# One output DMA per result tile, with a re-ordered first stage, in a fused attention and hard-swish MLP kernel

## Chip, cores and metric

The kernel runs on one core of a Trainium2 chip. The metric is device time in microseconds (us). The kernel before was timed three times; the profile is one further execution. A core has five engines, each with a queue of its own that is worked through in order: TensorE (PE, with its weight loads as PEld), VectorE (DVE), ScalarE (ACT), GpSimd (POOL), and SyncE (SP), which here only issues DMA transfers. The transfers are carried out by 16 DMA engines.

## What is computed

Cosine attention over 8 batches of 12 heads (448 positions, 64 channels), and then a two-layer MLP on the 3,584 tokens:

```python
q_n = q / (norm(q, axis=-1) + 1e-6)          # q, k, v: (8, 12, 448, 64) float32
k_n = k / (norm(k, axis=-1) + 1e-6)
attn = softmax(q_n @ k_n.T / tau)
x = (attn @ v) -> (8 * 448, 12 * 64)
h = x @ w_in                                 # (768, 2048)
g = h * clip(h + 3, 0, 6) / 6
out = g @ w_out                              # (2048, 768), out: (3584, 768) float32
```

## The kernel before

The work is cut into 48 **pairs** of heads, six to a batch. For each pair, q and k are loaded (`LQ`, line 174), squared (`SQ`, 203 or 201), summed (`RE`, 215), turned into reciprocal norms on ACT (`NO`, 231 to 234), multiplied (`NM`, 246), and transposed, on PE (`TR`, 291) in the first pairs and by a DMA transpose later (`XD`, 302). PE makes the scores in four groups (`SC`, 394), ACT the exponentials (`EX`, 412), PE the product with v (`VA`, 433), DVE the division (`FI`, 448). The result goes back into channel-major form by PE (`BK`, 466, with a copy `CX`) or by a DMA transpose (`XB`, 480). v is loaded by `LV` (four transfers, 186) and cast by `VC`.

When the six pairs of a batch are in `xT`, the first product of the MLP can run: 16 **units** per batch of six matmuls each (`mm1_unit`, 496), with a Relu on ACT (505) and a product on DVE (511) behind each. The second product is 56 units of 16 matmuls (`mm2_unit`, 532). One such unit makes a tile of 128 tokens by 384 columns. `store` copies it out of PSUM into `o` (543 on ACT, 545 on DVE, in turn; four buffers) and sends it to `out`. The weights come in eight transfers issued by POOL (`W`, 591).

The 128 rows of a tile are not consecutive tokens. Token `7 p + c` of a batch sits at place `p` of chunk `c`, and a tile holds two chunks of 64 tokens, so its rows lie 7 rows apart in `out`, in two groups. For tiles 0 to 2 of a batch the groups are two neighbouring chunks of one batch; tile 3 (odd batches only) takes chunk 6 of two batches. The kernel before sends each group by a DMA of its own:

```python
for e in range(2):
    ...
    eng = nc.scalar if end == 1 and e else nc.sync
    eng.dma_start(out=r[:, cols], in_=o[64 * e : 64 * e + 64, 0:width])
```

The last unit of all is cut into two halves of 192 columns, and one of its four transfers is issued by ACT.

The order of the work is written out by hand. For pairs 0 to 17, `PLAN` is a list of short names (`SQ.1.a.0.4` is a square of item 1 on ACT, `U` one MLP unit, `UA` and `UV` its ACT and DVE halves, `DP.n` a run of n matmuls on zeros that keep PE occupied). Each engine executes its share in the order of this list. `ORDER` says which kind of unit (first or second product) each of the first 36 `U` takes. From pair 18 on (`FIRST`) a loop emits one pair after the other: scores, exponentials, the values of the pair before, `XB`, `XD`, units, loads.

Of the kernel before, what the change touches and what calls it, by code (L numbers as in the profile page):

```python
# [15 lines left out]


FIRST = 18
ORDER = "111111111111111111111111111112212222"

PLAN = [
    "DP.4 LQ.1 DP.2 SQ.1.a.11.3 SQ.1.a.0.4 LQ.0 DP.2 LQ.3 SQ.1.a.4.3 DP.5 LQ.2 SQ.0.a.8.6 SQ.0.p.6.2 DP.4",
    "SQ.1.v.7.4 SQ.0.p.0.6 DP.3 RE.1.1 RE.1.0 RE.0.1 DP.1 NO.0.1 LQ.5 DP.4 RE.0.0 SQ.3.a.0.7 DP.2 NO.0.0 NM.1.v.0",
    "NM.0.p.1 DP.8 NM.1.v.1 SQ.2.a.0.7 RE.3 LQ.4 SQ.5.a.0.7 TR.1.Y DP.11 RE.2 NM.0.p.0 SQ.4.p.0.7 CK.0.v TR.0.Z",
    "NO.1 DP.2 CQ.0.v SC.0.0.0 RE.5 DP.3 DP.2 EX.0.0 SC.0.1.1 EX.0.1 DP.3 SC.0.2.0 LV.0 LQ.8 CK.1.v RE.4 LQ.7",
    "EX.0.2 CQ.1.v VC.0.p NM.2.p LQ.6 DP.6 SC.0.3.1 VA.0.0 NM.3.p LV.1 VC.1.v VA.0.1 SC.1.0.0 EX.0.3 VA.0.2 TR.2.Z",
    "VA.0.3 DP.3 SC.1.1.1 LV.2 NO.2 EX.1.0 FI.0 TR.3.Y SC.1.2.0 LQ.9 EX.1.1 NM.4.p CK.2.v VA.1.0 EX.1.2 CQ.2.v",
    "VA.1.1 VC.2.v SC.1.3.1 CQ.3.v NM.5.p SQ.7.p.0.7 SC.2.0.0 DP.2 EX.1.3 VA.1.2 EX.2.0 SC.2.1.1 EX.2.1 CK.3.v",
    "VA.1.3 SC.2.2.0 TR.4.Y BK.0.Z FI.1 SC.2.3.1 DP.2 EX.2.2 DP.1 EX.2.3 CQ.4.v SQ.6.p.0.7 W CX.0.v SC.3.0.0",
    "EX.3.0 CQ.5.v RE.7 TR.5.Z VC.3.v SC.3.1.1 VA.2.0 W VA.2.1 EX.3.1 VA.2.2 VA.2.3 RE.6 CK.4.v SQ.9.a.0.7",  # L30
    "SC.3.2.0 EX.3.2 SC.3.3.1 D.10 LQ.10 LQ.11 SC.4.0.0 CK.5.v FI.2 VA.3.0 NO.3 RE.9 SQ.8.p.0.7 NM.7.p EX.3.3",
    "BK.2.Z RE.8 EX.4.0 SC.4.1.1 VA.3.1 EX.4.1 SC.4.2.0 VA.3.2 EX.4.2 BK.1.Y CX.2.v VA.3.3 SC.4.3.1 LV.3 SC.5.0.0",
    "VC.4.v NM.6.p DP.2 EX.4.3 SC.5.1.1 EX.5.0 TR.7.Z CX.1.v TR.6.Y LV.4 EX.5.1 FI.3 SC.5.2.0 VC.7.p VA.4.0 EX.5.2",
    "VC.6.v CK.6.v NO.4 SC.5.3.1 VA.4.1 EX.5.3 VA.4.2 VC.5.p CS.6.v VA.4.3 DP.5 CQ.6.v CQ.7.v SQ.11.p.0.7 OPEN",
    "SQ.10.p.0.7 CS.7.v CK.7.v FI.4 RE.11 SC.6.0 SC.6.1 EX.6.0 EX.6.1 BK.3 SC.6.2 VA.5.0 NM.8.p VA.5.1 EX.6.2",
    "CX.3.v VA.5.2 VA.5.3 FI.5 SC.6.3 SC.7.0 SC.7.1 TR.8 XB.4 EX.6.3 VA.6.0 LQ.13 VA.6.1 EX.7.0 RE.10 NM.9.p",
    "SC.7.2 EX.7.1 CQ.9.v VA.6.2 EX.7.2 BK.5 TR.9 CQ.8.v LQ.14 CX.5.v SC.7.3 VA.6.3 VC.9.p CK.9.v U NO.5 FI.6 U U",
    "UA UA VA.7.0 EX.7.3 VA.7.1 UA CS.9.v UV W CS.8.v CK.8.v SC.8.0 UV UV SC.8.1 NM.10.p VA.7.2 VA.7.3 FI.7 EX.8.0",
    "SC.8.2 LQ.12 VC.8.p W EX.8.1 TR.10 U LV.5 EX.8.2 UA VA.8.0 CQ.11.v SC.8.3 SQ.13.p.0.7 VA.8.1 CQ.10.v UV",
    "SC.9.0 SC.9.1 EX.8.3 NM.11.p EX.9.0 RE.13 VA.8.2 SC.9.2 VA.8.3 FI.8 EX.9.1 SC.9.3 LQ.15 EX.9.2 U UA TR.11",  # L40
    "SQ.12.p.0.7 EX.9.3 RE.12 CS.11.v VA.9.0 VA.9.1 VC.10.p U CK.10.v XB.6 NO.6 NM.12.p VC.11.p SQ.15.p.0.7",
    "CK.11.v SC.10.0 CS.10.v UV VA.9.2 U UA SC.10.1 EX.10.0 UV UA EX.10.1 SC.10.2 VA.9.3 EX.10.2 LV.6 U UV UA",
    "TR.12 LQ.17 LQ.16 CQ.12.v XB.7 SC.10.3 U SQ.14.p.0.7 NM.13.p UV CQ.13.v SC.11.0 UA RE.15 FI.9 EX.10.3 EX.11.0",
    "U U UV UA UA VA.10.0 SC.11.1 EX.11.1 UV SC.11.2 EX.11.2 VA.10.1 UV VA.10.2 TR.13 SC.11.3 LQ.19 U LV.7 CS.12.a",
    "UA VA.10.3 RE.14 NO.7 SQ.17.p.0.7 NM.15.p CS.13.v CK.13.a U U FI.10 EX.11.3 UA VA.11.0 VA.11.1 VA.11.2",
    "NM.14.p SQ.16.a.0.7 UA CK.12.v SC.12.0 RE.17 XB.8 UV W U VA.11.3 VC.12.p U UV UV EX.12.0 FI.11 SC.12.1 UA",
    "XB.9 UV VC.15.p UA UV EX.12.1 LQ.18 SC.12.2 XB.10 VA.12.0 BK.11 SC.12.3 SC.13.0 EX.12.2 CX.11.v VA.12.1 XD.15",
    "U EX.12.3 EX.13.0 SC.13.1 SC.13.2 UA W U EX.13.1 VA.12.2 RE.16 SQ.19.p.0.7 VC.13.a VA.12.3 EX.13.2 UV SC.13.3",
    "UA U XD.14 FI.12 NO.8 UV SQ.18.p.0.7 CK.14.v U U EX.13.3 U VA.13.0 UA UV SC.14.0 UA UA UA EX.14.0 UV CS.14.v",
    "VC.14.a UV UV SC.14.1 EX.14.1 U SC.14.2 UA NM.16.v RE.19 UV EX.14.2 VA.13.1 U UA U W VA.13.2 UA RE.18 UV UV",  # L50
    "CK.15.v U LQ.20 SC.14.3 UA NO.9 XD.16 UV LQ.21 VA.13.3 U FI.13 U U NM.17.p XD.17 XB.13 UA VA.14.0 UV VA.14.1",
    "SC.15.0 UA EX.14.3 XB.12 VA.14.2 LV.8 UV UA UV EX.15.0 VA.14.3 SC.15.1 W EX.15.1 SC.15.2 FI.14 SQ.21.a.0.7",
    "CK.16.v EX.15.2 SC.15.3 SQ.20.a.0.2 U EX.15.3 U VA.15.0 SQ.20.p.2.5 VA.15.1 NM.19.v RE.20 UV SC.16.0 VC.17.v",
    "CS.16.v SC.16.1 UA CK.17.v SC.16.2 XD.19 EX.16.0 VC.16.v VA.15.2 RE.21 LQ.22 VA.15.3 U EX.16.1 EX.16.2",
    "SC.16.3 FI.15 UA NM.18.p U UV U XD.18 EX.16.3 UA NO.10 VA.16.0 VA.16.1 SC.17.0 SQ.22.p.0.7 SC.17.1 LV.9",
    "VC.18.p UV CK.18.v RE.22 EX.17.0 SC.17.2 VA.16.2 NM.20.v LV.11 XB.14 EX.17.1 VA.16.3 U LQ.23 VC.19.a SC.17.3",
    "UA U EX.17.2 FI.16 XB.16 UV CK.19.v LV.10 CS.18.v EX.17.3 VA.17.0 XB.15",
]


# [1 line left out]
def kernel(  # L62
# [10 lines left out]
    nc = tc.nc  # L73
    B, H, S, D = q.shape
    d_model, d_ff = moe_w_in.shape
# [194 lines left out]
    def bank_of(name, reads):  # L270

        bank = {"Y": Y, "Z": Z}[name] if name else next_bank()
        key = id(bank)
        assert not unread.get(key), name
        unread[key] = reads
        return bank, key
# [246 lines left out]
    def mm2_unit(b, t, m, end=None):  # L523
        assert not weights
        g = gT[(b // 2) % 2]
        ps, key = bank_of(None, 1)
        width = MH if end is None else MH // 2
        cols = slice(m * MH + width * (end or 0), m * MH + width * (end or 0) + width)
        for fc in range(FCN):
            c0 = (S + SR) * (b % 2) + 128 * t if t < 3 else SM  # L530
            lhs = g[:, fc, c0 : c0 + 128]
            nc.tensor.matmul(  # L532
                ps[:, 0:width],
                lhs,
                w_out_sb[:, fc, cols],
                start=(fc == 0),
                stop=(fc == FCN - 1),
            )

        def store():  # L540
            o = sb.tile([128, MH], FP32, name="o", tag="o", bufs=4)
            if on_act:
                nc.scalar.copy(out=o[:, 0:width], in_=ps[:, 0:width])  # L543
            else:
                nc.vector.tensor_copy(out=o[:, 0:width], in_=ps[:, 0:width])  # L545
            unread[key] = 0
            for e in range(2):
                if t < 3:
                    r = out[b * S : (b + 1) * S].rearrange("(p c) m -> c p m", c=7)[2 * t + e + b % 2]
                else:  # L550
                    r = out[(b - 1 + e) * S : (b + e) * S].rearrange("(p c) m -> c p m", c=7)[6 * (1 - e)]
                eng = nc.scalar if end == 1 and e else nc.sync
                eng.dma_start(out=r[:, cols], in_=o[64 * e : 64 * e + 64, 0:width])

        evac_n[0] += 1
        on_act = evac_n[0] % 2 == 1
        post["a" if on_act else "v"].append(store)

    def second(b):
# [107 lines left out]
    SC = [psum_s.tile([128, 2, 512], FP32, name=f"SC{n}", tag=f"SC{n}") for n in range(2)]  # L667
# [3 lines left out]
    by_kind = {"1": [u for u in stream if u[0] is mm1_unit], "2": [u for u in stream if u[0] is mm2_unit]}  # L671
    first = [by_kind[x].pop(0) for x in ORDER]
    stream = first + [u for u in stream if u not in first]
# [91 lines left out]
```

## Time and profile before

| | before |
|---|---|
| timed runs | 428.23 us median (426.42, 428.23, 429.01) |
| profiled run | 424.55 us; 422.8 us from the first to the last instruction |
| PE busy | 411.1 us, 97% of the span |
| ACT, DVE, POOL busy | 271.2, 217.7, 181.1 us |
| output transfers | 110 of 96 KB and 4 of 48 KB, 2.2 us to landing |
| read from and written to memory | 47.19 MB and 11.01 MB |

The page lists each engine's busy time, the same in 40 slices of the span, and the chain of work that ended last. A group line reads: source line, engine, operation, output from inputs, count, then busy time and the mean duration in ns. A windows line gives a stretch of time, then for each engine its busy time and the instructions, then the granted TensorE clock, the mean busy share of the 16 DMA engines, and the rate in GB/s at which they moved data.

### The profile page before, as it was taken

To read this page: it belongs to the slowest core of one execution; us is meant where nothing else is said; L and a number is where in the kernel's file an instruction comes from. 1 tells how busy PE (TensorE), PEld (TensorE's weight loads), DVE (VectorE), ACT (ScalarE), POOL (GpSimd) and SP (SyncE) were. 2 spreads that over 40 slices of the span, in tenths; PEclk is the share of its full clock that TensorE was granted. 3 is DMA by queue.
4 is the path that set the end of the run, shared out by engine and by line. 5 is a ranking of instruction groups with operands and counts; after the bars stand their busy time and mean duration, and the time that the engine had idled before them with its cause. 6 is when DMAs were issued, how large, how long until landed. Compare 5 with 4: busy or idle time off the path is not lost.

```text
span 422.8 us, 9251 instructions
## 1 busy us (share of the span) xinstructions
PE 411.1 (97%) x3574; PEld 243.2 (58%) x3575; DVE 217.7 (52%) x419; ACT 271.2 (64%) x593; POOL 181.1 (43%) x184
## 2 busy tenths in 40 slices
PE   6999999999997999999999999999999999999996
PEld 5556655556654555656555555555555555655564
DVE  7689777675443454465455454554554343214410
ACT  6899989977555765866756775676765675105400
POOL 5997787512235456365365464374472200000000
PEclk9999999999999999999999999999999999999999
DMA  8997999996879767676995856668666251330033
GB/s 287 307 244 201 243 194 226 220 194 145 210 170 203 174 175 138 167 194 127 179 193 136 183 156 156 158 154 188 164 160 95 63 75 33 70 75 19 2 75 76
DMA packets 94156, 65.82 MB, mean 156 GB/s; under 512 B 58656, under 2 KB 92576, under 8 KB 94112
## 3 DMA queue, kind: packets, MB, share of 16 engines
q1 hardware_dynamic: 90320, 58.89, 60.4%
q0 software_dynamic: 3712, 6.29, 8.7%
q8 instruction: 28, 0.46, 0.5%
q14 instruction: 16, 0.13, 0.1%
q10 hardware_dynamic: 80, 0.05, 0.0%
HBM read 47.19 MB, written 11.01 MB: 138 GB/s over the span
## 4 chain that ended last, share of the span: by engine, by line
PE 88%; ACT 4%; DMA 4%; SPq 2%; issue 1%; POOL 0%; DVE 0%; ACTq 0%; POOLq 0%
PE M L496 22%; PE M L532 22%; PE PV L433 11%; PE Y L496 6%; PE M L394 6%; PE Z L496 5%; PE Y L532 5%; PE Z L532 5%; ACT at L412 3%; DMA tT<-nrm 2%; PE Z L394 2%; DMA raw<-in_k_dram 1%; PE SC L394 1%; PE Y L394 1%; PE PV L603 1%; DMA vr<-in_v_dram 1%
## 5 line engine op out<-in xcount | busy, mean ns | idle before, releaser
L532 PEld LDWEIGHTS <-gT 128*128 128x128 bf16 x912 | 88.7, 98 | 58.6
L412 ACT ACTIVATE at<-M 128x448 bf16<-128x448 f32 x195 | 94.9, 568 | 30.5 <-PE M L394 25.3
L496 PEld LDWEIGHTS <-w_in_sb 128*128 128x128 bf16 x768 | 74.1, 98 | 67.1 <-issue 3.4
L532 PE MATMUL M<-w_out_sb,gT 128*128 128x384 bf16 (+1 forms) x640 | 106.0, 322 | 0.0
L496 PE MATMUL M<-xT,w_in_sb 128*128 128x448 bf16 x510 | 104.2, 352 | 0.0
L246 POOL TENSOR_TENSOR nrm<-raw,r 128x896 bf16<-128x896 f32 (+1 forms) x45 | 74.2, 1655 | 26.6 <-ACT r L234 22.9
L203 POOL TENSOR_TENSOR sq<-raw 128x896 f32<-128x896 f32 (+3 forms) x42 | 67.8, 1618 | 28.9 <-DMA raw<-in_k_dram 11.6
L511 DVE SCALAR_TENSOR_TENSOR gT<-u,M 128x448 bf16<-128x448 bf16 x85 | 52.5, 621 | 51.0 <-ACT u L505 49.8
L505 ACT ACTIVATE u<-M,half_bias 128x448 bf16<-128x448 f32 x85 | 55.1, 652 | 20.9 <-PE M L496 19.5
L433 PEld LDWEIGHTS <-at 128*128 128x128 bf16 x1344 | 53.3, 98 | 24.9 <-issue 17.7
L433 PE MATMUL PV<-vx,at 128*128 128x65 bf16 (+1 forms) x1344 | 63.9, 198 | 0.0
L215 DVE TENSOR_REDUCE n<-sq 128x14 f32<-128x896 f32 (+1 forms) x50 | 51.9, 1041 | 3.4 <-POOL nrm L246 2.0
L351 POOL COPY km<-tT 64x128 bf16<-64x128 bf16 x34 | 10.6, 312 | 94.1 <-DVE rc L448 33.7
L543 ACT COPY o<-M 128x384 f32<-128x384 f32 (+1 forms) x21 | 9.9, 471 | 40.9 <-PE M L532 40.9
L449 DVE TENSOR_TENSOR on<-PV,rc 128x512 bf16<-128x512 f32 x48 | 33.2, 692 | 3.5 <-DMA xT<-on 1.9
L545 DVE COPY o<-M 128x384 f32<-128x384 f32 (+1 forms) x19 | 10.4, 547 | 47.7 <-PE M L532 47.7
L394 PE MATMUL M<-tT,kz 64*128 64x448 bf16 (+1 forms) x172 | 33.4, 353 | 1.4 <-DMA tT<-nrm 0.5
L412 ACT ACTIVATE at<-Y 128x448 bf16<-128x448 f32 x48 | 27.4, 571 | 10.9 <-PE Z L394 10.9
L412 ACT ACTIVATE at<-Z 128x448 bf16<-128x448 f32 x51 | 29.0, 569 | 3.0 <-PE M L394 2.7
L496 PE MATMUL Y<-xT,w_in_sb 128*128 128x448 bf16 x138 | 29.9, 352 | 0.0
L448 DVE RECIPROCAL rc<-PV 128x8 f32<-128x8 f32 x48 | 9.9, 206 | 38.2 <-PE PV L433 34.9
L496 PE MATMUL Z<-xT,w_in_sb 128*128 128x448 bf16 x120 | 26.1, 352 | 2.0 <-DMA xT<-on 2.0
(78 smaller groups left out, 342.8 us busy)
## 6 DMA issues: line engine op xcount, KB each, us to landing
vr<-in_v_dram SPq DMA_DIRECT2D x96, 128.0 KB, 3.8
raw<-in_k_dram SPq DMA_DIRECT2D x24, 448.0 KB, 4.4
raw<-in_q_dram SPq DMA_DIRECT2D x24, 448.0 KB, 4.3
out_dram<-o SPq DMA_DIRECT2D x110, 96.0 KB, 2.2
w_in_sb<-in_moe_w_in_dram POOLq DMA_DIRECT2D x4, 768.0 KB, 12.1
w_out_sb<-in_moe_w_out_dram POOLq DMA_DIRECT2D x4, 768.0 KB, 11.2
xT<-on SPq DMA_TRANSPOSE x42, 3.8
tT<-nrm SPq DMA_TRANSPOSE x34, 2.9
```

What stands on the lines that cost most here:

```text
L203: engines[e].tensor_tensor(out=o, in0=i, in1=i, op=ALU.mult)
L215: nc.vector.tensor_reduce(out=n2s[d % 2][:, j % 2, c], in_=sq[:, :, :, :].rearrange("p g c d -> p (g c) d")[:, c, :], axis=AX.X, op=ALU.add,)
L246: engines[e].tensor_tensor(out=nrm[:, :, g, :].rearrange("p c g d -> p g c d"), in0=raw_of[j][:, g, :, :], in1=rs[d % 2][3][:, j % 2, :] . ...
L351: nc.gpsimd.tensor_copy(out=km[p, :, p], in_=z[p, 3, :, :])
L394: nc.tensor.matmul(o, ks, qt[rows], start=True, stop=True)
L412: nc.scalar.activation(out=o, in_=x, func=AF.Exp, scale=inv_tau)
L433: nc.tensor.matmul(o, at[:, n, q_cols(i // HP, j)], mv, start=(name == "A0" and j % 2 == 0), stop=last, skip_group_check=True,)
L449: nc.vector.tensor_tensor(out=on[:, :, :, :].rearrange("p (b j) h d -> p b (j h) d", b=2), in0=pv4[:, :, :, 0:D], in1=rc[:, :, :].to_broad ...
L496: nc.tensor.matmul(ps[:, 0:S], w_in_sb[:, cc, fc * 128 : (fc + 1) * 128], x[:, cc, 0:S], start=(cc == 0), stop=(cc == CC - 1),)
L505: nc.scalar.activation(out=u[:, :], in_=ps[:, 0:S], func=AF.Relu, bias=half_bias[:, :], scale=1.0 / 6.0)
L511: nc.vector.scalar_tensor_tensor(out=g[:, fc, c0 : c0 + S], in0=u[:, :], scalar=1.0, in1=ps[:, 0:S], op0=ALU.min, op1=ALU.mult,)
L532: nc.tensor.matmul(ps[:, 0:width], lhs, w_out_sb[:, fc, cols], start=(fc == 0), stop=(fc == FCN - 1),)
```

## The change

The two output transfers of a tile become one, whose destination is written as an access pattern with the two groups as its outermost dimension. `step` is the distance between the groups: one row for two neighbouring chunks, `S - 6` rows for the tile that spans two batches. All of them are issued by SyncE. What it is for: half as many output transfers to issue. The plan for pairs 0 to 17 is also replaced by another order of the same work, found by a search that took several lengths for the transfers.

```diff
-ORDER = "111111111111111111111111111112212222"
+ORDER = "111111111111111111111111111111222222"
 PLAN = [
-    "DP.4 LQ.1 DP.2 SQ.1.a.11.3 SQ.1.a.0.4 LQ.0 DP.2 LQ.3 SQ.1.a.4.3 DP.5 LQ.2 SQ.0.a.8.6 SQ.0.p.6.2 DP.4",
-    "SQ.1.v.7.4 SQ.0.p.0.6 DP.3 RE.1.1 RE.1.0 RE.0.1 DP.1 NO.0.1 LQ.5 DP.4 RE.0.0 SQ.3.a.0.7 DP.2 NO.0.0 NM.1.v.0",
-    "NM.0.p.1 DP.8 NM.1.v.1 SQ.2.a.0.7 RE.3 LQ.4 SQ.5.a.0.7 TR.1.Y DP.11 RE.2 NM.0.p.0 SQ.4.p.0.7 CK.0.v TR.0.Z",
+    "LQ.0 SQ.0.p.0.6 DP.2 DP.4 DP.1 LQ.1 DP.7 DP.2 DP.2 SQ.1.p.7.4 DP.5 SQ.0.v.6.2 DP.2 SQ.0.a.8.6 DP.3 D.10 LQ.2",
+    "DP.3 RE.0.1 SQ.1.a.4.3 RE.0.0 LQ.3 LQ.5 LQ.4 SQ.1.a.0.4 SQ.1.v.11.3 NO.0.0 RE.1.0 SQ.2.p.0.7 RE.1.1 RE.2",
+    "NM.0.p.0 LQ.6 DP.5 NM.0.p.1 LV.0 SQ.3.a.0.7 TR.0.Z NO.0.1 SQ.4.a.0.7 NM.1.p.0 RE.3 NM.1.v.1 DP.4 NO.1 CQ.1.v",
     ...
 ]
 ...
-            for e in range(2):
-                if t < 3:
-                    r = out[b * S : (b + 1) * S].rearrange("(p c) m -> c p m", c=7)[2 * t + e + b % 2]
-                else:
-                    r = out[(b - 1 + e) * S : (b + e) * S].rearrange("(p c) m -> c p m", c=7)[6 * (1 - e)]
-                eng = nc.scalar if end == 1 and e else nc.sync
-                eng.dma_start(out=r[:, cols], in_=o[64 * e : 64 * e + 64, 0:width])
+            c = 2 * t + b % 2 if t < 3 else 6
+            row = b * S + c if t < 3 else (b - 1) * S + c
+            step = 1 if t < 3 else S - 6
+            r = bass.AP(
+                tensor=out.tensor,
+                offset=out.offset + row * d_model + cols.start,
+                ap=[[step * d_model, 2], [7 * d_model, 64], [1, width]],
+            )
+            nc.sync.dma_start(out=r, in_=o[:, 0:width])
```

In the rest of the new plan the `XB` of pairs 1 and 2 stand in place of PE's `BK` of 1 and 2, `BK` of pairs 4 and 8 in place of `XB` of 4 and 8, and the weight transfers `W` come earlier. The number of `U` is 36 in both plans, and the loop from pair 18 on is unchanged.

## The prediction

> **What bounds the kernel now.** I read the page's busy times first, then PE's waits, then the chain in order of time, and last the DMA engines by stage.
>
> PE's waits, from the list of who waited for whom (engine and line, what it waited for, us in total, times, longest):
>
> ```profile
> PE Z L496 <- DMA xT<-on: 2.0, 1, 2.0
> PE M L394 <- DMA tT<-nrm: 0.5, 1, 0.5
> ```
>
> The page has PE busy for 97%, but in the first 41 us many of its matmuls are the zero runs of lines 603 and 598 (77 and 9 of them), which compute nothing. The first unit of the MLP starts at 41 us; until then ACT is busy 23.5 of the 25 us from 15 to 40. From 136 us to the last matmul at 419 us PE streams without a gap: a first-product unit takes 1.14 us, a second-product unit 2.60, again and again in the chain. So PE's own work sets the end, plus what PE loses before 136 us. The two waits above are the whole of the loss after 126 us. Both are for transfers that SyncE issued late. Its timeline (start us, us, line, operation, transfer, count) has no gap from 99 to 127 us:
>
> ```profile
> 119.21 1.17 SPq L553 DMA_DIRECT2D out_dram<-o  x2
> 120.43 2.67 SPq L186 DMA_DIRECT2D vr<-in_v_dram  x4
> 123.15 1.28 SPq L480 DMA_TRANSPOSE xT<-on  x1
> 124.47 0.59 SPq L174 DMA_DIRECT2D raw<-in_k_dram  x1
> 125.17 1.20 SPq L480 DMA_TRANSPOSE xT<-on  x1
> ```
>
> The last line is the transpose that PE waits for until 129.1 us. The 12 output transfers issued between 99.3 and that line held SyncE for 8.6 us (3.67 + 1.17 + 1.19 + 1.42 + 1.17).
>
> The DMA engines by stage (stretch, five engines' busy time, clock, **DMA share**, **GB/s**):
>
> ```profile
> 5.00:10.00 5.00, 4.32 (x42) 3.54 (x40) 4.34 (x8) 4.41 (x13) 2.13 (x4) 1.00 1.03 380
> ```
>
> ```profile
> 100.00:160.00 60.00, 57.38 (x496) 33.76 (x492) 28.79 (x51) 36.45 (x84) 23.43 (x23) 1.00 0.74 179
> 160.00:320.00 160.00, 160.00 (x1388) 94.13 (x1385) 81.07 (x144) 107.07 (x243) 83.47 (x80) 1.00 0.72 163
> 320.00:361.00 41.00, 41.00 (x350) 23.96 (x348) 16.76 (x32) 26.29 (x56) 6.22 (x9) 1.00 0.40 61
> ...
> 400.00:423.00 23.00, 19.04 (x133) 12.35 (x131) 2.03 (x4) 2.23 (x5) 0.00 (x0) 0.97 0.28 70
> ```
>
> The reader should see two prices. From 5 to 10 us only loads run: 380 GB/s over 16 engines busy 1.03 of the time is 380 / 16.5 = 23.1 GB/s for an engine while it is busy. From 400 us on only outputs run: 70 / (16 x 0.28) = 15.6 GB/s. And from 100 to 320 us the engines are already busy for 0.72 to 0.74 of the time with everything spread over all 16.
>
> [...] when loads pile up at 38 to 57 us, a transpose of `xT` issued at 42.77 lands 15.2 us later, against a median of 3.8. [...] Issue time is what merging saves here: the trace has about 0.6 us for each transfer.
>
> **The change part by part.**
>
> *Fewer issues.* 114 output transfers become 57. Ahead of the late transpose six of 12 go, about 4.3 us of SyncE time. It is issued at 120.9 in place of 125.2 and lands at about 124.8, while PE wants it at 127. Both waits go: 2.0 + 0.5, with the gaps around them 2.8 us. Elsewhere SyncE's time is hidden behind PE.
>
> *The merged transfer.* Its destination has dimensions 2 x 64 x 384, its source 128 x 384. [...] each output tile runs on **two DMA engines** in place of 16, the same two each time, 64 rows of 1,536 bytes (98.3 KB) on each. At 23.1 GB/s that takes 98.3 / 23.1 = 4.26 us, at 15.6 GB/s 6.3 us. The trace shows no write at such a width, so these are my two bounds. I take 4.5 us, near the lower, since the 15.6 was measured with 16 engines writing at once and here two do.
>
> *Those two engines from 100 us to 361 us.* 42 of the 56 units of the second product lie there (84 transfers before). Their outputs need 42 x 4.5 = 189 us of each of the two engines. The rest of the traffic still takes its sixteenth. Upper bound from busy shares: 60 x 0.74 + 160 x 0.72 + 41 x 0.40 = 176 us per engine, less the outputs' part before (84 x 98.3 KB = 8.26 MB at 15.6 GB/s over 16 engines = 33 us), is 143 us. Lower bound from bytes at the loads' rate: 10.7 + 26.1 + 2.5 - 8.3 = 31 MB, over 16 engines at 23.1 GB/s, 84 us. I take the middle, 113.5. Sum 302.5 us in a stretch of 261: 41.5 us too much. The four `o` buffers allow four tiles of backlog (18 us), which drain from 361 to 400 us, where only six units store. The other 23.5 us reach PE, in two ways: the copies behind the second product wait for a free `o`, on ACT and DVE in turn, and behind them in those queues stand exponentials and Relus, for which PE waits; and loads and transposes, which need all 16 engines, stand in the rings behind outputs. This is **+23.5 us**.
>
> *The end.* From 398 us the last eight units run at 2.60 us each, faster than two engines take their tiles. Of the 2.2 us to landing now, 98.3 KB at 16 x 15.6 GB/s are 0.4 and latency 1.8. So the first store moves from 402.9 (matmuls done 400.6, copy 0.5, latency 1.8). Seven tiles x 4.5 and two halves x 2.3 make 36.1 us, so the last lands at 439.0, against 421.7 before: **+17 us**. PE is done by then.
>
> *The new order.* The same 36 units and within 1 us the same work on ACT, DVE and PE by its end; weights leave earlier and two of the early transposes move from PE to DMA. On POOL a full square (line 203, 1.68 us) now stands ahead of the first products with the norms, and ACT squares item 4, whose load lands only at 11.0 us, ahead of the second norms and of item 5 (0.95 us). So the first exponentials start some 1.6 us later than the 12.4 of before. On the other side ACT has about 1.5 us less to do ahead of the values of pair 5. I cost the order at nothing (-2 to +2): ACT bounds this stage in both. Sixteen more matmuls on zeros (1.7 us) stand where PE waits for the first norms anyway.
>
> Sum: 428.2 - 2.8 + 23.5 + 17 = **466 us**.
>
> **The rivals.**
>
> *Sixteen engines all the same.* If the hardware spreads the merged pattern over 16 engines, only the saved issues remain: 428.2 - 2.8 - 1 (some of the 1.9 to 4.5 us by which the timed runs exceed the profiled one may be such waits) = 424.4, not slower. For it: nothing in the trace contradicts it, and the bytes and row lengths are unchanged. [...]
>
> *Two engines, hidden until the end.* With 4.26 us and 84 us: 179 + 84 = 263 of 261, which the backlog absorbs. Only the end remains, 7 x 4.26 + 2 x 2.2 = 34 from 402.9, +15: 428.2 - 2.8 + 15 = 440. For it: in the saturated start an engine does reach 23 GB/s. Against it: the busy share is far above what bytes alone explain, as the transposes move in small packets.
>
> *Two engines at the price of now.* 42 x 6.3 = 265, + 143 = 408, 147 too much, less 25 of backlog: +122. The end: 7 x 6.3 + 2 x 3.2 = 50.5 from 402.9, +31. 428.2 - 2.8 + 122 + 31 = 578. For it: 15.6 GB/s is the only measured price of such a write. Against it: each engine would write at half the rate at which it reads.
>
> **How the numbers follow.** Two engines as reckoned 0.54, hidden until the end 0.24, the price of now 0.10, sixteen engines 0.12. The predicted time is 466. The range leaves out the sixteen and most of the dear case: from 434, a little under the cheap case, to 545. Faster than 1% needs sixteen engines and a good order (0.05); within 1%, 0.07; slower 0.88.
>
> **What would show it.** Right: output transfers that land in 6 us or more in place of 2.2; a DMA share that stays as it is while loads and transposes land late; new waits of ACT and DVE copies (543, 545) for `o`, and PE gaps after 136 us; and 10 us or more between the last matmul and the end. Each step has its mark: no gap near 129 us for the saved issues, the tail for the end. Wrong: landings near 2.5 us and a PE without gaps. Then the time lies near 424, or the order decides it.

## The result, and the profile after

| | before | changed |
|---|---|---|
| median of the timed runs | 427.78 us (4 runs) | 475.71 us (472.92 to 477.99) |
| ratio | | 1.112, 95% interval 1.105 to 1.119 |
| span of the profile | 422.8 us | 471.1 us |
| from the last matmul to the end | 3.7 us | 17.6 us |
| output transfers | 114 | 57 |

The change made the kernel 11% slower. The time of a kernel, above and below, is the median over its executions in the faster of the two states that they fall into; one of 16 executions with shared buffers and two of the four with a wide end (467.9 and 470.4 us) were in the slower one and are left out.

First the list of PE's waits in the changed kernel (engine and line, what it waited for; us in total, times, longest):

```profile
PE M L496 <- DMA xT<-on: 11.2, 2, 7.3
PE M L394 <- DMA tT<-nrm: 9.3, 6, 2.8
PE Z L394 <- DMA tT<-nrm: 4.4, 2, 2.2
...
PE Y L496 <- DMA xT<-on: 2.3, 1, 2.3
```

The reader should see that the two waits of before have become eleven, 27.2 us in place of 2.5, and that all are for the same two kinds of DMA transpose. None is for an output. Next the stages of the changed kernel (stretch, busy time of PE, PEld, DVE, ACT and POOL, clock, DMA share, GB/s):

```profile
100.00:160.00 60.00, 50.48 (x414) 29.09 (x413) 23.14 (x41) 32.10 (x74) 19.63 (x20) 0.91 0.89 119
160.00:320.00 160.00, 146.30 (x1243) 84.73 (x1241) 72.59 (x127) 95.93 (x216) 73.04 (x69) 0.98 1.01 147
320.00:361.00 41.00, 36.67 (x311) 21.61 (x309) 18.90 (x34) 23.89 (x56) 19.12 (x20) 1.00 1.09 127
...
434.00:471.00 37.00, 19.49 (x136) 12.60 (x134) 2.03 (x4) 2.24 (x5) 0.00 (x0) 0.80 0.12 43
```

The DMA share goes up from 0.72 to 1.01 between 160 and 320 us while the rate falls from 163 to 147 GB/s: the packets take longer. Those of 256 bytes, which are the transposes', take 58 ns in the mean in place of 24, at an unchanged median of 18, so some of them wait long. From 434 us on only outputs move, one queued behind the other, and the share is 0.12. Times 16 that is 1.9: as much as two engines busy and 14 idle. The rate of 43 GB/s over 1.9 engines is 22 GB/s each.

The number of engines can also be counted. The trace has 5,472 completion marks for the 342 transfers of the kernel before, 16 each. The changed kernel has 3,819 for 285. Its 228 other transfers take 3,648 of them, so its 57 outputs have 171, three each. On each of the eight semaphores that SyncE's transfers count on, 13 marks are missing for each output, so the shortage is the outputs' alone. The packets agree. Beside its rows an output has packets of 4 bytes. In the kernel before there are 16 of them: the one output on ACT's queue has 80 packets, 64 of them rows. With the same rows, loads and transposes the queues q1 and q10 carry 90,400 packets there and 88,690 in the changed kernel; the difference of 1,710 is 114 x 16 less 57 x 2, so two are left for each output. (The profile gives no time to landing for SyncE's transfers here, since it counts to 16.)

Last, SyncE's own timeline where the longest wait arises (start, us, line, operation, transfer, count), from the changed kernel:

```profile
122.62 2.41 SPq L174 DMA_DIRECT2D raw<-in_k_dram  x1
125.14 3.92 SPq L480 DMA_TRANSPOSE xT<-on  x1
129.15 3.02 SPq L302 DMA_TRANSPOSE tT<-nrm  x1
132.27 2.33 SPq L555 DMA_DIRECT2D out_dram<-o  x2
134.71 4.67 SPq L302 DMA_TRANSPOSE tT<-nrm  x1
```

Issuing has become slow by itself. A load took 0.6 us and a transpose 1.2 before; here they take 2.4 and up to 4.7. Over the whole run that is true of the `tT` transposes above all. Their issues, before and then changed (count, then shortest, median and longest in ns, first and last start in us):

```profile
L302 SPq DMA_TRANSPOSE tT<-nrm x34: 1220/1252/2477, 68.3 to 337.6; - x34
L302 SPq DMA_TRANSPOSE tT<-nrm x34: 1221/2330/4674, 68.8 to 371.5; - x34
```

The median went from 1.25 to 2.33 us. That of the `xT` transposes rose only from 1.22 to 1.30, and that of the outputs stayed at 0.58.

### The profile page after: what moved, and what is told of

It reads as the page before. It is cut to its first block, busy times and chain, and to the rows that moved or that the text cites. A ratio compares the mean times of both kernels' runs of the same rounds, so it can differ in the third digit from the quotient of the medians.

```text
span 471.1 us, 9209 instructions
## 1 busy us (share of the span) xinstructions
PE 420.2 (89%) x3591; PEld 246.8 (52%) x3591; DVE 218.0 (46%) x420; ACT 272.2 (58%) x588; POOL 180.5 (38%) x187
## 3 DMA queue, kind: packets, MB, share of 16 engines
q1 hardware_dynamic: 88690, 58.94, 76.1%
HBM read 47.19 MB, written 11.01 MB: 124 GB/s over the span
## 4 chain that ended last, share of the span: by engine, by line
PE 69%; DMA 22%; ACT 2%; DVE 1%; SPq 1%; issue 1%; POOL 0%; ACTq 0%; POOLq 0%
PE M L496 18%; PE M L532 16%; DMA tT<-nrm 15%; PE PV L433 8%; PE M L394 5%; PE Z L496 5%; PE Y L532 4%; DMA xT<-on 4%; PE Y L496 3%; PE Z L532 3%; DMA out_dram<-o 2%; ACT at L412 2%; PE PV L605 1%; PE Z L394 1%; DMA raw<-in_q_dram 1%; PE Y L394 1%
## 5 line engine op out<-in xcount | busy, mean ns | idle before, releaser
L412 ACT ACTIVATE at<-M 128x448 bf16<-128x448 f32 x200 | 97.0, 564 | 42.0 <-PE M L394 35.1
L496 PE MATMUL M<-xT,w_in_sb 128*128 128x448 bf16 x510 | 110.8, 367 | 11.2 <-DMA xT<-on 11.2
L496 PEld LDWEIGHTS <-w_in_sb 128*128 128x128 bf16 x768 | 75.3, 100 | 84.1 <-issue 24.1
L532 PE MATMUL M<-w_out_sb,gT 128*128 128x384 bf16 x592 | 101.2, 327 | 0.0
L203 POOL TENSOR_TENSOR sq<-raw 128x896 f32<-128x896 f32 (+2 forms) x39 | 63.8, 1635 | 28.1 <-DMA raw<-in_q_dram 27.0
L412 ACT ACTIVATE at<-Z 128x448 bf16<-128x448 f32 x47 | 26.5, 564 | 11.6 <-PE M L394 8.7
L543 ACT COPY o<-M 128x384 f32<-128x384 f32 x18 | 8.7, 482 | 41.2 <-PE M L532 41.2
L545 DVE COPY o<-M 128x384 f32<-128x384 f32 x19 | 10.6, 557 | 46.6 <-PE M L532 42.2
L532 PE MATMUL Y<-w_out_sb,gT 128*128 128x384 bf16 (+1 forms) x192 | 31.9, 319 | 0.0
L496 PE MATMUL Z<-xT,w_in_sb 128*128 128x448 bf16 x144 | 31.4, 354 | 0.0
```

The lines of the kernel that those rows point to most:

```text
L203: engines[e].tensor_tensor(out=o, in0=i, in1=i, op=ALU.mult)
L412: nc.scalar.activation(out=o, in_=x, func=AF.Exp, scale=inv_tau)
L496: nc.tensor.matmul(ps[:, 0:S], w_in_sb[:, cc, fc * 128 : (fc + 1) * 128], x[:, cc, 0:S], start=(cc == 0), stop=(cc == CC - 1),)
L532: nc.tensor.matmul(ps[:, 0:width], lhs, w_out_sb[:, fc, cols], start=(fc == 0), stop=(fc == FCN - 1),)
```

## The experiments

The leading theory: the outermost dimension of 2 confines each output to two DMA engines; their queue delays the transposes that PE needs, and holds up the end. The rivals: merging by itself costs, or the new order does.

**The order alone.** The changed kernel with the two transfers of before:

```diff
-            c = 2 * t + b % 2 if t < 3 else 6
...
-            nc.sync.dma_start(out=r, in_=o[:, 0:width])
+            for e in range(2):
...
+                eng = nc.scalar if end == 1 and e else nc.sync
+                eng.dma_start(out=r[:, cols], in_=o[64 * e : 64 * e + 64, 0:width])
```

> The new order of pairs 0 to 17, with two output transfers for each tile as before. Two-engine theory: the loss is the transfers' alone, so this stays with the kernel before: 425 to 430 us, no PE wait over 2 us after 140 us, last landing about 2.5 us after the last matmul. Rival, the order is what costs: 470 or more. Rival in between, each has a share: 440 to 460.

Measured: 423.38 us against 427.01, ratio 0.993 (0.990 to 0.995). The order costs nothing and gains 0.7%, a little more than the theory's own range allowed. Its longest PE waits, apart from one of 2.5 us for `vx` at the start, which every version has:

```profile
PE SC L394 <- ACT at L412: 0.7, 1, 0.7
PE M L496 <- DMA xT<-on: 0.6, 1, 0.6
```

With 114 outputs still to issue, the late transposes of the old order are all but gone. So the order cures them by itself.

**Merging alone.** The kernel before, with the changed kernel's transfer and its old order:

```diff
-            for e in range(2):
...
+                ap=[[step * d_model, 2], [7 * d_model, 64], [1, width]],
+            )
+            nc.sync.dma_start(out=r, in_=o[:, 0:width])
```

> The old order with one transfer for each tile, outermost dimension 2. Two-engine theory: 470 to 480 us, packets of output at about 65 ns, PE waits for late transposes from 130 us on, 14 us between the last matmul and the end. Rival, the order costs: 428.

Measured: 484.45 us, ratio 1.134 (1.127 to 1.142), above the range expected, with 29.4 us of waits for transposes and 17.6 us from the last matmul to the end. The loss is the transfer's. The old order suffers more from it than the new one (475.7).

**Two transfers, nothing merged, 2 x 32 rows each.** This and the next were meant to separate merging from the number of engines:

```diff
-                eng.dma_start(out=r[:, cols], in_=o[64 * e : 64 * e + 64, 0:width])
+                r = r[:, cols].rearrange("(k n) m -> k n m", k=2)
+                eng.dma_start(out=r, in_=o[64 * e : 64 * e + 64, 0:width])
```

> The kernel before with its two transfers for each tile, nothing merged; only the destination of each is written as 2 x 32 x 384 in place of 64 x 384. Two-engine theory: the same 64 rows of each tile fall on each of two engines, so it is as slow as the merged kernel, 470 to 485 us, with 10 us or more from the last matmul to the end. Rival, the merging itself costs (a larger transfer that lands later and holds its buffer longer): 428 us, since nothing is merged.

Measured: 428.05 us, ratio 1.003. With 4 in place of 2:

> As the run with halves of 2, with the destination as 4 x 16 x 384. Two-engine theory: four engines carry the outputs, 2.1 us for each tile, 89 us in the stretch from 100 to 361 us, which with 84 to 143 us of other traffic fits in 261; and 2.1 is under the 2.6 us of a unit, so no queue builds up at the end: 427 to 433 us. Were the loss in proportion to the width (half of what two engines lose), it would be about 450.

Measured: 429.01 us, ratio 1.005 (1.002 to 1.007). Taken at their word these would sink the theory, but they are no test of it. The two new dimensions have one common stride, and the builder joins them: the instruction carries 64 x 384, as before, and the trace has 16 marks for each of the 342 transfers and 2.2 us to landing. Both are the kernel before once more; what they show is that 0.5% between such runs means little, so the 0.7% of the order alone is not far above it.

**The same with strides that can't be joined.** The 64 rows are dealt out in turn:

```diff
+                r = r[:, cols].rearrange("(n k) m -> k n m", k=2)
+                eng.dma_start(out=r, in_=o[64 * e : 64 * e + 64, 0:width])
```

> Old order, two transfers for each tile as in the kernel before, but the 64 rows of each are taken as 2 x 32 rows that are dealt out in turn (outermost step one row, inner step two), which can't be joined into one dimension. The rows of out are permuted within each group of 64; bytes, rows and number of transfers are those of the kernel before. Two-engine theory: as slow as the merging alone, 478 to 492 us, since 64 rows of each tile again fall on each of two engines. Rival, the merging costs: 427 us.

Measured: 493.61 us, ratio 1.152 (1.145 to 1.158), just over the range. Nothing is merged, the bytes and the number of transfers are those of the kernel before, and it is the slowest of all: 34.1 us of waits for transposes, 17.9 us at the end. Its 114 outputs have 338 marks, three each but for four, and the one on ACT's queue has 66 packets, two beside its 64 rows. After the last matmul the stages read:

```profile
480.00:492.00 12.00, 0.00 (x0) 0.00 (x0) 0.00 (x0) 0.00 (x0) 0.00 (x0) 0.50 0.12 43
```

Again 0.12 of 16 engines, 43 GB/s. So the number of engines is the cause and merging isn't.

**Four engines.** The same edit with `k=4`.

> The same with 4 x 16 rows. Two-engine theory: four engines, 2.1 us for each tile on each, 89 + (84 to 143) us of work in a stretch of 261 and 2.1 us against a unit of 2.6 at the end: no overload, 427 to 433 us. Rival, loss in proportion to the width: about 455.

Measured: 434.55 us, ratio 1.014 (1.009 to 1.020), 1.6 us over the first range and far from 455. The marks are five for each output (570 for 114), and the output on ACT's queue has four packets beside its 64 rows, against two in the run above and 16 in the kernel before, which fits four engines. PE waits 5.3 us for transposes, and the end takes 5.8 us. Twice the engines took away nearly all of the loss here, as from an overload, and not a part in proportion.

**Half as many transfers, another way.** Both units of a tile share one buffer of 768 columns, and 64 whole rows go out at once:

```diff
-            o = sb.tile([128, MH], FP32, name="o", tag="o", bufs=4)
+                    o_of[b, t] = [sb.tile([128, d_model], FP32, name="o", tag="o", bufs=2), 0]
...
+                    eng.dma_start(out=r, in_=o[64 * e : 64 * e + 64, :])
```

> New order; the number of output transfers is halved in another way: the two units of a tile (384 columns each) share one buffer of 768 columns, of which there are two, and each group of 64 rows goes out in one transfer of 64 rows of 3,072 bytes behind the second unit, so the outermost dimension stays 64. The last tile goes as before. Two-engine theory: no loss, 421 to 424.5 us; against the order alone (423.4) little is to be gained, since only 0.6 us of PE's waits there were for transfers. Rival, that larger transfers cost by themselves (they land later and hold their buffer longer): 430 or more.

Measured: 424.5 us, ratio 0.993 (0.990 to 0.995), with 2.7 us to landing. Large transfers on 16 engines didn't hurt here; nor did they gain over the order alone (423.4 us).

**Only the end.** The changed kernel, with the merged transfer for the last batch alone:

```diff
+            if b == B - 1:
                 c = 2 * t + b % 2 if t < 3 else 6
...
+            else:
+                for e in range(2):
```

> New order; only the tiles of the last batch (the last eight units) use the merged transfer, the others two as before. Two-engine theory: only the end is paid, 14 us: 435 to 440 us, with PE without gaps until its last matmul. Rival, the end hides under other costs or needs the backlog of the earlier tiles: 425 to 430.

Measured: 437.11 us, ratio 1.023 (1.018 to 1.029), 13.7 more than the order alone (about 13 by their ratios to the kernel before, as the two come from different chips). PE has 0.5 us of waits for transposes; the end takes 17.7 us. After the last matmul:

```profile
419.00:435.00 16.00, 0.00 (x0) 0.00 (x0) 0.00 (x0) 0.32 (x1) 0.00 (x0) 0.61 0.12 45
```

**Merged, with 64 outermost.** One transfer for each tile, the two dimensions exchanged:

```diff
-                ap=[[step * d_model, 2], [7 * d_model, 64], [1, width]],
+                ap=[[7 * d_model, 64], [step * d_model, 2], [1, width]],
```

> New order and one transfer of 192 KB for each tile, as in the changed kernel, with the two dimensions of the destination exchanged: 64 x 2 x 384 in place of 2 x 64 x 384. The rows of out are permuted within a tile; bytes, rows and number of transfers are those of the changed kernel. Two-engine theory: [...] the whole loss goes, 421 to 425 us, landing about 2.7 us. Rival, one merged transfer for each tile costs by itself: 440 or more.

Measured: 422.33 us, ratio 0.989 (0.988 to 0.991). All that the changed kernel loses is gone with this one line; the issue table for the outputs of this run and the stages:

```profile
out_dram<-o SPq DMA_DIRECT2D x55, 192.0 KB, 2.3
```

```profile
160.00:320.00 160.00, 160.00 (x1392) 94.03 (x1391) 81.56 (x144) 106.61 (x242) 82.61 (x79) 1.00 0.68 162
...
400.00:421.00 21.00, 16.97 (x121) 11.08 (x118) 2.03 (x4) 1.76 (x4) 0.00 (x0) 1.00 0.21 76
```

The transfer of 192 KB lands in 2.3 us, hardly later than one of 96 KB in the kernel before (2.2 us), and PE has no gap between 160 and 320 us. All 285 transfers have 16 marks. In the last stretch, where outputs alone move, an engine moves 76 / (16 x 0.21) = 22.6 GB/s while it is busy: as fast as the two engines of the changed kernel, and faster than the 15.6 GB/s of the kernel before.

**The same with the old order.**

> The same transfer with the old order. If the saved issues on SyncE are worth the two waits near 129 and 135 us (2.8 us), this is 424 to 426 us against 427.8 of the kernel before, and the wait of line 496 for the transpose is gone. If they are worth nothing, 427 to 428.5.

Measured: 423.22 us against 426.61, ratio 0.991 (0.988 to 0.994). The waits for transposes are gone here too, so halving the issues is worth some 3 us to the old order. The figure is rough, since kernels with the same instructions differed by up to 2.0 us above.

**Another queue.** The changed kernel with ACT issuing the outputs:

```diff
-            nc.sync.dma_start(out=r, in_=o[:, 0:width])
+            nc.scalar.dma_start(out=r, in_=o[:, 0:width])
```

> The changed kernel with its output transfers issued by ACT in place of SyncE: still two engines and the same work for them, but in the rings of ACT's queue, so that loads and transposes don't stand behind outputs in one ring. If the order within the rings is what delays the transposes: 440 to 450 us (the end's 14 us, and some waits for o). If the two engines' capacity is the limit whatever the ring: 465 to 485 us, with waits of the copies for o in place of those for transposes.

Measured: 461.06 us, ratio 1.080 (1.077 to 1.083), between the two forecasts. The 11.01 MB of output now move on a queue of their own, and PE's waits for transposes fall from 27.2 to 3.0 us, so most of those waits go with standing in the same DMA queue as the outputs. But a new wait takes their place in part. ACT, which must now wait for the copies of DVE before it can issue, holds back its exponentials:

```profile
ACT at L412 <- DVE o L545: 6.9, 1, 6.9
```

PE's last matmul ends at 442.1 us, against 453.5 in the changed kernel and 417.0 with 64 outermost, so two thirds of PE's loss stay, and PE's listed waits past the start (7.9 us) are less than half of what stays. How much of it is the engines' capacity and how much ACT's wait for the copies, this run doesn't tell.

**All but the end.** The reverse of the run above (`if b < B - 1`).

> The changed kernel with two transfers for each tile of the last batch (eight units), merged for all others. If the two terms of the loss add up: 475.7 less 14, 460 to 464 us, with the last landing about 3 us after the last matmul.

Measured: 458.8 us from two executions (458.08 and 459.56), a little under the range and 16.9 less than the changed kernel, with 27.1 us of waits for transposes as there, and 3.7 us at the end. The two terms add up to within about 3 us: 423.4 + 13.7 + (458.8 - 423.4) = 472.5, against 475.7.

The fastest kernel with its rows in place is the new order with two transfers for each tile (423.4), level with the shared buffers (424.5). The exchanged dimensions (422.3) can't be told from it: their ratios to the kernel before, 0.988 to 0.991 and 0.990 to 0.995, overlap. They leave the rows of a tile permuted; to put them in place the columns of `gT` would have to be interleaved, and that wasn't tried.

## Why the prediction was right

The forecast was 466 us, the measurement 475.7, inside the range. The mechanism held, two engines and a queue on them. That the sum came within 10 us is in part luck: the stage from 100 to 361 us was 13 us too small, while the end was 3 us too large and the new order's gain of 3.6 us was left out. With the measured terms the sum is 427.8 - 3.6 + 36.6 + 13.9 = 474.7.

**Two engines.** Shown by the packets of 4 bytes (two for each output with 2 outermost, four with 4, 16 in the kernel before), by the marks (three, five and 16), by the share of 0.12 when outputs run alone, and by the pair of runs that differ in one line (475.7 and 422.3). That 2 outermost would mean two engines was an assumption of mine: in the trace of before every transfer has 16 marks. The rival of sixteen engines fell.

**The price of a tile, 4.5 us.** A row of 1,536 bytes takes 65 ns at the median in the changed kernel's trace, so 64 rows one after the other take 4.2 us; in the last stage whole outputs end 3.9 us apart. The lower bound of 4.26 was the right one, and the rival at 6.3 us fell with this. The reason given for it was wrong. I put the 15.6 GB/s down to 16 engines writing at once, but with 64 outermost 16 engines write at once too, and the row takes the same 65 ns. The slow rows, 107 ns at the median, are those of the kernel before and of the order alone, where a transfer of 64 rows from 64 partitions is spread over 16 engines. Why they are slow stays open.

**The end, +17 us.** Measured 13.7 (run with only the end merged) and 13.9 (17.6 less 3.7 in the profiles). The mechanism held, the size was a little high.

**From 100 to 361 us, +23.5 us.** The stage was right and the size too small. By profiles of the same order, the changed kernel loses 36.6 us on PE after 126 us that the 64-outermost version doesn't (sum of the gaps beyond each matmul's usual spacing). Waits make up 28.7 of these: 27.2 for transposes, 1.5 for a sum on DVE. Most of the other 8 are PE's clock, for which the working had no term: four stretches at half clock. Stages of the changed kernel around the longest wait:

```profile
127.00:132.00 5.00, 0.67 (x4) 0.23 (x3) 0.51 (x1) 1.38 (x4) 0.00 (x0) 1.00 1.58 98
132.00:139.00 7.00, 4.02 (x12) 1.67 (x12) 1.11 (x2) 1.73 (x5) 2.26 (x3) 0.51 1.36 94
139.00:146.00 7.00, 4.78 (x52) 3.03 (x51) 2.27 (x5) 2.61 (x7) 2.60 (x3) 0.98 0.53 163
146.00:149.00 3.00, 3.00 (x12) 1.39 (x11) 0.90 (x2) 2.09 (x5) 3.00 (x3) 0.50 1.00 285
```

PE waits from 127.7 to 135.0. Its clock is at half from 132.0 to 138.9 us, and again from 145.7 to 149.1, after a wait of 2.2 us. Of the four stretches three last 3.4 us and one 6.8. They have about 14 us in which PE works, and half of that is lost. That they come after waits of PE is what the trace shows (see the last section); what sets them off it doesn't show.

The way to PE was only half right, too. I named two: copies that wait for a free `o`, and transposes that stand behind outputs in the DMA queue. The second is what the trace shows in the late transposes, and the run with the outputs on ACT's queue, where such waits are 3.0 us in place of 27.2, speaks for it. The copies wait for an output three times, 15.9 us in all: 4.0 us until 124.8 us, only 0.1 us past the last matmul that this copy needs, and 11.9 at 454 and 458 us, when only the end is behind them. No wait of PE is put down to any of the three. So the kernel did not run on a full backlog of four tiles through this stage, as the sum had it; a few transposes landed late instead. Of the signs that I named, the late transposes, the gaps of PE and the end came true; the DMA share did not stay but rose, and the gap near 129 us did not go but grew to 7.3 us. The landings of the outputs can't be read.

**Fewer issues, -2.8 us.** Right where all 16 engines are used (-3.4 us in the old order). In the changed kernel it came to nothing, since the transposes took longer to issue behind the queue. The cause of the two old waits was SyncE's backlog, as read; but the new order removes them as well, so the two gains don't add (422.3, 423.2 and 423.4 us). From 99 to 127 us, with the two transfers for each tile in both orders, SyncE issues 9 loads in the new order and 15 in the old.

**The order at nothing, -2 to +2.** Measured -3.6 us. The later first exponentials came true in part (13.0 us against 12.4, where I had 1.6 more). What I missed was the order of SyncE's queue from 90 us on.

## What to carry to other kernels

Before merging transfers, look at the outermost dimension of the access pattern: in the destination it, not the size, decided how many DMA engines carried a transfer here. With 2, 4 and 64 outermost they were two, four and sixteen (2, 4 and 16 packets of 4 bytes for each output). The DMA share of a stretch in which one kind of transfer runs alone, times 16, is the mean number of busy engines. It tells how many engines carry the transfer only if the next is always queued: 0.12 with the queue of the changed kernel means two, but 0.21 with 64 outermost means 3.4 and not sixteen. The completion marks told them apart either way: three, five and 16 for each output. The queue on two of the engines was paid here by transposes, which have 16 marks each, and the few late ones cost PE more (36.6 us) than the sum of mean loads had given (23.5).

## What the runs showed that was not expected

- Some PE waits cost more than their length: the clock was at half after them. In the changed kernel the four stretches at half clock begin at 132.0, 145.7, 193.5 and 302.7 us, all on one grid of 3.41 us. In the 3.41 us just before them PE had been idle for 3.4, 2.2, 3.4 and 2.3 us of the 3.4. A wait of 2.9 us until 327.5 us fell across two steps of the grid, at most 1.9 us in one, and no slow stretch followed it. A few cases like these give no exact limit.
- With the backlog on two engines the issuing of transposes was slower: `tT` took 2.33 us to issue in place of 1.25. With the outputs on ACT's queue it still took 2.03, and with 64 outermost 1.27, so the slow issue goes with the load on the two engines and not with the shared queue alone.
- Merging made writes faster where all 16 engines carried them: 65 ns for a row of 1,536 bytes with 64 outermost, against 107 in the kernel before. With two and four engines it was 65 too, also for 64 rows from 64 partitions.
